# Keys transposed into the raw weights' buffer, tokens loaded first in a segment, value tiles on alternating banks, and memory's answers behind the first projection

## The chip, the cores and the metric

The kernel runs on one core of a Trainium2 chip. The metric is the device time of one execution in microseconds. Before the change three runs gave a median of 693.09 us (692.84 to 693.54).

## The reference

One input x (2048 tokens, 448 features) is normalised and goes through two branches whose results are added to x: an attention with a compressive memory, and a gated linear unit. All is float32.

```python
xn = _layernorm(x)
return x + _A_ref(xn, wq, wk, wv, wo, beta) + _B_ref(xn, w_gate, w_up, w_down)

# A: 16 heads of 28, 4 segments of 512 tokens, one after the other
logits = einsum("bhqd,bhkd->bhqk", qs, ks) * scale + mask      # causal, inside a segment
a_dot = softmax(logits) @ vs
a_mem = (phi(qs) @ M) / (phi(qs) @ z + 1e-6)                   # memory of the earlier segments
o = g * a_mem + (1 - g) * a_dot                                # g = sigmoid(beta), per head
M += phi(ks)^T @ vs;  z += sum(phi(ks))                        # phi(t) = t + 1 or exp(t)
# B: h = sigmoid(xn @ w_gate) * (xn @ w_up);  h @ w_down       # 448 -> 1792 -> 448
```

## The kernel before, in words

Every large product is computed with each operand split into a high and a low part, so one 448-deep product is 11 matmuls (the list TERMS). The program has two stages.

The **front** (lines 282 to 645) goes through the four segments b = 0 to 3 of 512 tokens. In a segment, TensorE computes four value tiles of 128 tokens (`values`, 11 matmuls at L334 each); after the third it updates the memory with the keys and values of the segment before (`update`, 128 small matmuls at L399, reading kn and vst); then it recalls the memory for the queries of the segment before (`recall`, 32 matmuls at L420 on phi, then four DVE transposes at L423); then come seven projections c = 0 to 6 of 128 columns of keys and queries together (`keys_queries`, 11 matmuls at L359 each). Keys are columns 0 to 447, so projections 0 to 2 are keys, 3 is half keys, half queries, and 4 to 6 are queries. In the last segment the order is 3, 4, 5, 6, 0, 1, 2. Between the projections stand the transposes of the next segment's tokens (L97).

What follows each projection: ScalarE copies the high part (L360) and computes the two first steps of phi into a tile e (L364, L365); DVE subtracts for the low part (L366) and finishes e (L368). The pair of parts goes to DRAM (qd, L372). Where the columns are keys, `turn_keys` transposes e in 32 by 32 blocks into a tile `tb` (L383) and four transfers write it to DRAM (kd, L386), from where kn is loaded in token order (L390), in two pieces, after projections 3 and 4. Where the columns are queries, e goes to DRAM (fd, L371), and after projection 6 `phi_queries` loads phi from there in four transfers (L411). The stores of qd for projections 5 and 6 are held back until phi's loads are issued.

The recalled answers of the segment before are handled one per projection: `divide` (DVE L131 to L133, then a multiplication on GpSimd, L134), and one projection later `answer`: a DVE transpose into a `tb` buffer (L430) and a store that GpSimd issues (od, L431).

Buffers around the change: `tb` has three buffers, for keys and answers together; e has three; `stage` is an 8 KB tile that holds the raw weights of projections 0 to 3 at the start and nothing afterwards. The eight PSUM banks are shared by tag: "p", "s" and "gu" two banks each, "m" and "pd" one each. In the first three segments projections use "p" and "gu" by turns, in the last "p" and "s"; value tiles 0 and 1 use "p", 2 and 3 "gu" (in the last segment "s"). The bank of a projection is free when DVE has finished e from it.

The tokens of segment b + 2 (one load of 896 KB into acc, L617) are issued on SyncE after projection 2 of segments 0 and 1. Their first reader is `statistics` (L300) in the next segment.

In the last segment the first steps of the **joint stage** (the gated unit, attention's scores and weights, and the output projection, woven together by a count of steps) already stand between the projections.

In the front the order of TensorE, ScalarE, DVE and SyncE is the written one; GpSimd's is chosen by the planner. In the joint stage TensorE and SyncE keep the written order, and the planner orders the others. A buffer of a tag is chosen by the planner among those that it takes to be free; the first writer waits for the last reader of that buffer.

Of the kernel before, what the change touches and what calls it, by code (L numbers as in the profile page):

```python
# [9 lines left out]
F32 = mybir.dt.float32  # L10
# [6 lines left out]
P = 128  # L17
# [4 lines left out]
NB = 4  # L22
L = 512
# [3 lines left out]
HG = 4  # L27
NG = H // HG
# [35 lines left out]
def kernel(  # L64
# [10 lines left out]
    nc = tc.nc  # L75
# [8 lines left out]
    acc = [keep.tile([P, NT, D], F32, name=f"acc{b}") for b in range(NB)]  # L84
# [27 lines left out]
    def x_block(b):  # L112
        return x[b * L:(b + 1) * L, :].rearrange("(t p) d -> p t d", p=P)
# [5 lines left out]
    def bank(name, tag):  # L119
        return ps.tile([P, L], F32, name=name, tag=tag, bufs=banks[tag])  # L120
# [48 lines left out]
    rest, begin, wo = [], [], {}  # L169
# [112 lines left out]
    with tc.tile_pool(name="front", bufs=2) as sb, tc.manual_schedule(engines=FRONT):  # L282
        stage = eight_k(F32, "stage").rearrange("p (c a) n -> p c (a n)", c=4)
# [56 lines left out]
                nc.sync.dma_start(vd[b], vst.rearrange("p t h d -> p t (h d)"))  # L340

        def values(b, t):
            pv = bank("pv", "p" if t < 2 else "gu" if b < NB - 1 else "s")
            value_terms(b, t, pv, TERMS)
            turned.append(pv)
            if t == 2:
                update(b - 1)
            if t > 1:
                for n in range(len(turned)):
                    store_values(b, t + 1 - len(turned), turned.pop(0))  # L350

        turned = []

        def keys_queries(b, c):

            qk = four_k(F32R, "qk")
            pp = bank("pp", ("p", "gu" if b < NB - 1 else "s")[c % 2])
            for n, (a, w) in enumerate(TERMS):
                T.matmul(pp, wqk[c][:, w, :], xs[b][:, a, :], start=n == 0, stop=n == len(TERMS) - 1)  # L359
            A.activation(qk[:, 0, :], pp, AF.Copy)  # L360
            e = None
            if (c < 4 and b < NB - 1) or (c > 2 and b > 0):
                e = sb.tile([P, L], F32, name="e", bufs=3)
                A.activation(e, pp, AF.Relu, scale=-1.0)  # L364
                A.activation(e, e, AF.Exp, scale=-1.0)  # L365
            V.tensor_sub(qk[:, 1, :], pp, qk[:, 0, :].bitcast(F32))  # L366
            if e is not None:
                V.scalar_tensor_tensor(e, pp, 0.0, e, op0=ALU.max, op1=ALU.add)  # L368
                if c > 2 and b > 0:
                    lo = max(c * P - D, 0)  # L370
                    nc.sync.dma_start(fd[b][lo:(c + 1) * P - D], e[D + lo - c * P:])  # L371
            held.append(lambda: nc.sync.dma_start(qd[b][c * P:(c + 1) * P], qk.bitcast(F32)))  # L372
            if c < 5 or b == 0:
                held.pop()()
            elif c == 6 and b < NB - 1:
                phi_queries(b)
            return e

        def turn_keys(b, c, e):

            n = min(P, D - c * P)
            kt = sb.tile([P, L], F32, name="tb", bufs=3)
            V.transpose(kt[:n], e[:n])  # L383
            for f in range(0, n, 32):
                rows = kd[b][:, c * P + f:c * P + f + 32].rearrange("(t r) k -> r t k", r=32)
                nc.sync.dma_start(rows, kt[f:f + 32].rearrange("r (t k) -> r t k", k=32))  # L386
# [18 lines left out]

        phi_of, held = {}, []

        def phi_queries(b):
            phi_of[b] = sb.tile([P, HG, L], F32, name="phi", bufs=1)
            for i in range(NG):  # L410
                nc.sync.dma_start(phi_of[b][32 * i:32 * i + DH],  # L411
                                  fd[b][i * GW:(i + 1) * GW].rearrange("(j p) n -> p j n", p=DH))
            while held:
                held.pop(0)()

        def recall(b, phi, tag="s"):
            n2 = [bank("n2", t) for t in (tag, tag, "pd", "m")]
            for j in range(HG):
                for i in range(NG):
                    T.matmul(n2[i][32 * j:32 * j + 32], mst[b % 2][32 * i:32 * i + DH, 32 * j:32 * j + 32],  # L420
                             phi[32 * i:32 * i + DH, j], start=True, stop=True, tile_position=(32 * i, 32 * j))
            for i in range(NG):
                V.transpose(phi[:, i], n2[i])  # L423

        def divide(i, phi):
            weigh(sb, phi[:, i], gate[:, i:i + 1], MEM_EPS)

        def answer(b, i, phi):
            tb = sb.tile([P, L], F32, name="e", bufs=3) if b == NB - 1 else sb.tile([P, L], F32, name="tb", bufs=3)
            V.transpose(tb, phi[:, i])  # L430
            nc.gpsimd.dma_start(od[b][P * i:P * (i + 1)], tb)  # L431

# [73 lines left out]
        pv = [bank("pv", t) for t in ("p", "p", "gu", "gu")]  # L506
# [57 lines left out]
        for b in range(NB):  # L564
            last = b == NB - 1
            xn = {}
            if b > 1:
                phi = phi_of[b - 1]
            st = None
            for t in range(3 if b == 0 else 0, NT):  # L570
                if b > 0:
                    values(b, t)
                if 0 < b < NB - 1 and t == 2:
                    st = rstd(*st)
                    for n in range(2):
                        xn[n] = normalise(b + 1, n, *st[n])
                if b > 1 and t == 3:
                    recall(b - 1, phi, "gu" if last else "s")
                    if last:
                        begin[3]()  # L580
                        divide(0, phi)
                if b == 0:
                    split_qk(t)
                if last and t == 0:
                    next(ffn)
                if last:
                    continue
                if t == (3 if b == 0 else 0):
                    st = statistics(b + 1, 0, NT)
                if t == (3 if b == 0 else 2):  # L590
                    A.activation(one, ident[:, 0:1], AF.Exp)
            e = {}
            for k, c in enumerate(LAST if last else range(7)):
                e[c] = keys_queries(b, c)
                if b == 0 and c + 4 < 7:
                    split_qk(c + 4)
                if k < 4 and not last:
                    turn_keys(b, c, e[k])
                if b > 1:
                    i = k + (1 if last else -1)  # L600
                    if 0 < i <= NG:
                        answer(b - 1, i - 1, phi)
                    if 0 <= i < NG:
                        divide(i, phi)
                if last and k == 3:
                    phi_queries(b)
                    phi = phi_of[b]
                if k == 0:
                    if b == 0:
                        st = rstd(*st)  # L610
                    if b == 0:
                        A.activation(gate, gate, AF.Exp, scale=-1.0)
                        V.tensor_scalar_add(gate, gate, 1.0)
                        V.reciprocal(gate, gate)
                        V.tensor_scalar(gate_n, gate, -1.0, 1.0, op0=ALU.mult, op1=ALU.add)
                if k == 2 and b < 2:
                    nc.sync.dma_start(acc[b + 2], x_block(b + 2))  # L617
                if last:
                    if k > 0:
                        next(ffn)  # L620
                    if k > 4:
                        begin[k - 5]()
                    continue
                if k == 3:
                    key_rows(b, 0, 3 * P)
                if k == 4:
                    key_rows(b, 3 * P, D)
                n = k - 1 if b == 0 else k + 1
                if 2 <= n < 6:
                    turn(b + 1, n - 2, xn[n - 2])  # L630
                if 0 <= n < 4 and n not in xn:
                    xn[n] = normalise(b + 1, n, *st[n])
                if b == 2 and k == 2:
                    next(ffn)
            if last:
                for i in range(2):
                    for _ in range(FILLS[i]):
                        next(ffn)
                    if i == 0:
                        recall(b, phi)  # L640
                        for j in range(NG):
                            divide(j, phi)
                    for j in range(2):
                        answer(b, 2 * i + j, phi)
                begin[2]()
# [3 lines left out]
    sb = ctx.enter_context(tc.tile_pool(name="att", bufs=1, reuse_waits="tile"))  # L649
# [207 lines left out]
    with tc.manual_schedule(engines=MANUAL), ExitStack() as joint:  # L857
        next(steps)
        k = sum(FILLS) + 6
# [51 lines left out]
```

## Time and profile before

| | |
|---|---|
| median of 3 runs | 693.09 us |
| profiled execution | 690.35 us, span 688.6 us |
| TensorE busy | 669.9 us (97%) |
| VectorE (DVE) busy | 561.5 us (82%) |
| ScalarE (ACT) busy | 335.0 us (49%) |
| GpSimd (POOL) busy | 169.8 us (25%) |
| mean granted TensorE clock | 0.994 |

Times in the profile are microseconds from the start of the span. PE is TensorE's matmuls, PEld its weight loads, SPq the issuing of transfers on SyncE. A row in order of time gives start, length, engine, line, operation, output and input, and in brackets the idle time before it with what ended it. A row of waits gives total, number and longest. In the chain of waits a row gives start, length and what the chain went through. The front ends at about 153 us; segment 1 starts at 38, segment 2 at 69 and segment 3 at 106 us.

### The profile page before, as it was taken

The numbers are of one execution on the slowest core, as the hardware profiler recorded it, in microseconds if no ns is written. First come the engines' busy times: TensorE is split into PE (matmuls) and PEld (weight loads), VectorE is DVE, ScalarE is ACT, GpSimd is POOL, SyncE is SP. The second block draws the span as 40 slices with busy tenths as digits, with TensorE's granted clock in tenths as the row PEclk, the third lists the DMA queues.
The fourth block names the chain that finished last, engine by engine and source line by source line (L and its number), as shares of the span: only waits on it lengthen the run. The fifth ranks groups of instructions, "written<-read, shape, count | busy, mean of one in ns | idle before, by whom it ended". The sixth has DMA issues, their size and how long they took to land.

```text
span 688.6 us, 11163 instructions
## 1 busy us (share of the span) xinstructions
PE 669.9 (97%) x3915; PEld 551.1 (80%) x3915; DVE 561.5 (82%) x979; ACT 335.0 (49%) x547; POOL 169.8 (25%) x368
## 2 busy tenths in 40 slices
PE   8999994999999999999999999999999999999998
PEld 8788673878778787887878778787887878778897
DVE  6857475457899899997998889899898899888964
ACT  5747362333464455544545555455544556544320
POOL 4402032213222232321331223222222233222000
PEclk9999998999999999999999999999999999999999
DMA  8678978788332432233441343324143423314272
GB/s 267 200 245 238 324 222 249 259 305 237 100 80 57 116 100 70 52 107 94 100 112 45 72 124 65 106 57 115 52 104 93 98 60 81 70 41 122 71 210 103
DMA packets 71567, 89.93 MB, mean 131 GB/s; under 512 B 30168, under 2 KB 46424, under 8 KB 71000
## 3 DMA queue, kind: packets, MB, share of 16 engines
q1 hardware_dynamic: 68504, 81.88, 40.7%
q0 software_dynamic: 3008, 7.34, 5.3%
q8 instruction: 31, 0.51, 0.3%
q14 instruction: 24, 0.20, 0.1%
HBM read 53.81 MB, written 35.39 MB: 130 GB/s over the span
## 4 chain that ended last, share of the span: by engine, by line
PE 82%; DMA 7%; DVE 6%; issue 2%; ACT 1%; POOL 1%; SPq 0%; DVEq 0%; POOLq 0%; ACTq 0%
PE pgu L252 38%; PE pd L178 19%; PE pa L755 5%; PE st L680 5%; PE po L844 5%; PE pp L359 5%; DMA kd<-tb 2%; PE pv L334 2%; DMA fd<-e 2%; DMA od<-tb 1%; PE pv L502 1%; DVE e L368 1%; DVE qk L366 1%; DMA kn<-kd 1%; DMA phi<-fd 1%
## 5 line engine op out<-in xcount | busy, mean ns | idle before, releaser
L252 PE MATMUL pgu<-xs,wgu 128*128 128x512 f32 x1232 | 315.0, 394 | 0.0
L252 PEld LDWEIGHTS pgu<-xs,wgu 128*128 128x128 f32 x1232 | 226.3, 188 | 44.0 <-issue 2.6
L178 PE MATMUL pd<-wdn,hh 128*128 128x448 f32 x672 | 161.5, 367 | 1.4 <-DVE acc L181 1.3
L695 POOL TENSOR_SCALAR_AFFINE_SELECT w<-w 128x256 f32<-128x256 f32 (+1 forms) x160 | 80.8, 507 | 234.8 <-ACT w L684 200.7
L178 PEld LDWEIGHTS pd<-wdn,hh 128*128 128x128 f32 x672 | 123.1, 188 | 16.9 <-DVE acc L181 1.9
L735 ACT ACTIVATE w<-w 128x1024 f32<-128x1024 f32 (+1 forms) x96 | 86.6, 914 | 87.2 <-DVE w L734 85.0
L734 DVE TENSOR_TENSOR w<-w,mb 128x1024 f32<-128x1024 f32 (+1 forms) x96 | 99.6, 1051 | 0.1
L684 ACT ACTIVATE w<-st 128x512 f32<-128x512 f32 x128 | 74.9, 588 | 47.0 <-PE st L680 45.2
L698 DVE TRANSPOSE_TENSOR_REDUCE mx<-w 128x32 f32<-128x1024 f32 x64 | 79.1, 1236 | 13.1 <-POOL w L695 13.0
L359 PE MATMUL pp<-xs,wqk 128*128 128x512 f32 x308 | 74.9, 395 | 0.0
L181 DVE TENSOR_TENSOR acc<-pd,acc 128x448 f32<-128x448 f32 x112 | 67.5, 603 | 1.4 <-PE pd L178 1.4
L359 PEld LDWEIGHTS pp<-xs,wqk 128*128 128x128 f32 x308 | 56.9, 188 | 13.2 <-issue 0.8
L680 PE MATMUL st<-qk 84*128 84x128 f32 (+3 forms) x256 | 63.9, 311 | 0.3 <-ACT w L684 0.2
L263 ACT ACTIVATE hh<-sg 128x512 fp32r<-128x512 f32 x56 | 35.1, 627 | 52.2 <-DVE sg L262 50.9
L680 PEld LDWEIGHTS st<-qk 84*128 84x128 f32 x256 | 48.2, 189 | 8.9 <-ACT w L684 1.3
L260 ACT ACTIVATE sg<-pgu 128x512 f32<-128x512 f32 x56 | 33.2, 592 | 37.5 <-PE pgu L252 36.3
L724 DVE STREAM_TRANSPOSE mb<-top 128x1024 f32<-128x1024 f32 x32 | 39.7, 1240 | 10.9 <-POOL top L721 10.5
L262 DVE SCALAR_TENSOR_TENSOR sg<-sg,pgu 128x512 f32<-128x512 f32 x56 | 37.3, 666 | 3.4 <-PE pgu L252 3.4
L334 PE MATMUL pv<-wv,xs 128*128 128x448 f32 x132 | 30.4, 385 | 9.9 <-DVE e L368 9.9
L267 DVE SCALAR_TENSOR_TENSOR hh<-sg,hh 128x512 fp32r<-128x512 f32 x56 | 38.6, 690 | 1.0 <-ACT hh L263 0.6
L755 PE MATMUL pa<-w,vv 128*32 128x128 f32 (+3 forms) x512 | 38.8, 436 | 0.0
L844 PE MATMUL po<-wo,xs 128*128 128x448 f32 (+2 forms) x187 | 36.3, 352 | 0.0
(100 smaller groups left out, 602.8 us busy)
## 6 DMA issues: line engine op xcount, KB each, us to landing
qk<-qd SPq DMA_DIRECT2D x192, 112.0 KB
qd<-qk SPq DMA_DIRECT2D x28, 512.0 KB
raw<-in_w_ffn SPq DMA_DIRECT2D x14, 512.0 KB
vd<-vst SPq DMA_DIRECT2D x4, 1024.0 KB
vv<-vd SPq DMA_DIRECT2D x16, 256.0 KB
od<-w POOLq DMA_DIRECT2D x16, 256.0 KB, 4.0
ob<-od SPq DMA_DIRECT2D x32, 128.0 KB
out<-acc SPq DMA_DIRECT2D x15, 224.0 KB
```

The lines of the kernel that those rows point to most:

```text
L178: T.matmul(pd[:, :D], l, r, start=n == 0, stop=n == len(mms) - 1)
L181: V.tensor_add(acc[b][:, t, :], pd[:, :D], acc[b][:, t, :])
L252: T.matmul(dst, wgu[f][:, w, side * P:(side + 1) * P], xs[b][:, a, :], start=n == 0, stop=n == len(TERMS) - 1)
L359: T.matmul(pp, wqk[c][:, w, :], xs[b][:, a, :], start=n == 0, stop=n == len(TERMS) - 1)
L680: T.matmul(st[:, at:at + L - kb * P], self.qk[:KS, 1, h, kb * P:(kb + 1) * P], self.qk[:KS, 0, h, kb * P:], start=True, stop=True)
L684: A.activation(w, st, AF.Copy)
L695: G.affine_select(d, d, pattern=pattern, base=0, channel_multiplier=-1, compare_op=ALU.is_ge, fill=MASK)
L698: V.tensor_reduce(mx[:, 16 * (n - 1):16 * (n + 1)], w3[:, n // 2, :2 * L].rearrange("p (b n) -> p b n", n=32), axis=mybir.AxisListType.X, ...
L734: V.tensor_sub(w, w, m)
L735: A.activation(w, w, AF.Exp, scale=SCALE)
L755: T.matmul(pa[32 * j:32 * j + 32, kb * P:], self.vv[:, kb, 32 * j:32 * j + 32], self.pairs[j // 2].block(j % 2, kb), start=kb == 0, stop=k ...
L844: T.matmul(po[:, cols], xs[b][:, a, t * P:(t + 1) * P], out_weights(w)[:, cols], start=m == 0, stop=m == len(TERMS) - 1)
```

## The change

Six things are edited.

1. `turn_keys` transposes into `stage[:, c, :]`, the quarter that held the raw weights of projection c. `tb` is then used by the answers alone and has two buffers instead of three; e has four instead of three.
2. The value tiles take the two tags by turns: "p", "gu", "p", "gu" (last segment: "p", "s", "p", "s").
3. The load of segment b + 2's tokens is issued before projection 0 instead of after projection 2.
4. The recall of the segment before moves from behind the last value tile to behind the matmuls of the first projection, ahead of what ScalarE and DVE do with that projection. In the last segment the first `divide` moves with it.
5. phi's loads 0 and 1 are issued before projection 6 of segments 1 and 2, loads 2 and 3 after it as before; in the last segment all four stay where they were.
6. The release of the held stores becomes a function of its own, called where it happened before.

```diff
         def values(b, t):
-            pv = bank("pv", "p" if t < 2 else "gu" if b < NB - 1 else "s")
+            pv = bank("pv", ("p", "gu" if b < NB - 1 else "s")[t % 2])
...
-        def keys_queries(b, c):
+        def keys_queries(b, c, between=None):
...
                 T.matmul(pp, wqk[c][:, w, :], xs[b][:, a, :], start=n == 0, stop=n == len(TERMS) - 1)
+            if between:
+                between()
             A.activation(qk[:, 0, :], pp, AF.Copy)
...
-                e = sb.tile([P, L], F32, name="e", bufs=3)
+                e = sb.tile([P, L], F32, name="e", bufs=4)
...
             elif c == 6 and b < NB - 1:
-                phi_queries(b)
+                phi_queries(b, 2, NG)
+                release()
...
-            kt = sb.tile([P, L], F32, name="tb", bufs=3)
+            kt = stage[:, c, :]
             V.transpose(kt[:n], e[:n])
...
+        def release():
+            while held:
+                held.pop(0)()
+
-        def phi_queries(b):
-            phi_of[b] = sb.tile([P, HG, L], F32, name="phi", bufs=1)
-            for i in range(NG):
+        def phi_queries(b, i0, i1):
+            if i0 == 0:
+                phi_of[b] = sb.tile([P, HG, L], F32, name="phi", bufs=1)
+            for i in range(i0, i1):
...
-            tb = sb.tile([P, L], F32, name="e", bufs=3) if b == NB - 1 else sb.tile([P, L], F32, name="tb", bufs=3)
+            tb = sb.tile([P, L], F32, name="e", bufs=4) if b == NB - 1 else sb.tile([P, L], F32, name="tb", bufs=2)
...
-                if b > 1 and t == 3:
-                    recall(b - 1, phi, "gu" if last else "s")
-                    if last:
-                        begin[3]()
-                        divide(0, phi)
+                if last and t == 3:
+                    begin[3]()
...
+            def recalls():
+                recall(b - 1, phi, "gu" if last else "s")
+                if last:
+                    divide(0, phi)
+
             e = {}
             for k, c in enumerate(LAST if last else range(7)):
-                e[c] = keys_queries(b, c)
+                if k == 0 and b < 2:
+                    nc.sync.dma_start(acc[b + 2], x_block(b + 2))
+                if 0 < b < NB - 1 and k == 6:
+                    phi_queries(b, 0, 2)
+                e[c] = keys_queries(b, c, recalls if b > 1 and k == 0 else None)
...
                 if last and k == 3:
-                    phi_queries(b)
+                    phi_queries(b, 0, NG)
+                    release()
                     phi = phi_of[b]
...
-                if k == 2 and b < 2:
-                    nc.sync.dma_start(acc[b + 2], x_block(b + 2))
```

More of the change, by code (lines that the diff above doesn't have):

```diff
@@ L406 @@
         phi_of, held = {}, []
-        def phi_queries(b):
-            phi_of[b] = sb.tile([P, HG, L], F32, name="phi", bufs=1)
-            for i in range(NG):
+        def release():
[5 more added lines that the diff above has]
+            for i in range(i0, i1):
                 nc.sync.dma_start(phi_of[b][32 * i:32 * i + DH],
                                   fd[b][i * GW:(i + 1) * GW].rearrange("(j p) n -> p j n", p=DH))
-            while held:
-                held.pop(0)()
         def recall(b, phi, tag="s"):
```

## The prediction

> **What bounds the kernel now.** I read the page first, then who waited for whom on PE, then PE, DVE and SyncE in order of time around the starts of the segments, and the chain of waits there.
>
> ```profile
> span 688.6 us, 11163 instructions
> PE 669.9 (97%) x3915; PEld 551.1 (80%) x3915; DVE 561.5 (82%) x979; ACT 335.0 (49%) x547; POOL 169.8 (25%) x368
> ```
> ```profile
> PE pv L334 <- DVE e L368: 9.9, 3, 7.9
> PE pmm L399 <- DMA kn<-kd: 1.3, 1, 1.3
> ```
>
> PE is the bound: 669.9 of 688.6 us busy. Nearly all that it waits for after the start lies in the attention front, at segment boundaries. In PE's order of time (start, length, instruction, idle before it):
>
> ```profile
> 46.51 0.98 PE L399 MATMUL pmm<-vst,kn 128*32 128x32 f32 x90 [1.33 <-DMA kn<-kd]
> 72.56 4.68 PE L334 MATMUL pv<-wv,xs 128*128 128x448 f32 x22 [0.97 <-DVE e L368]
> 80.81 2.87 PE L420 MATMUL n<-phi,mst 28*32 28x512 f32 x6
> 83.85 1.13 PE L420 MATMUL n<-phi,mst 28*32 28x512 f32 x26 [0.17 <-DMA phi<-fd]
> 84.91 5.33 PE L359 MATMUL pp<-xs,wqk 128*128 128x512 f32 x22
> 99.81 5.28 PE L359 MATMUL pp<-xs,wqk 128*128 128x512 f32 x22
> 106.08 2.48 PE L334 MATMUL pv<-wv,xs 128*128 128x448 f32 x11 [1.00 <-DVE e L368]
> 116.46 6.58 PE L334 MATMUL pv<-wv,xs 128*128 128x448 f32 x22 [7.89 <-DVE e L368]
> 126.61 1.14 PE L420 MATMUL n<-phi,mst 28*32 28x512 f32 x32
> ```
>
> Two losses are not printed as idle. The recall of segment 2 begins at 80.81 and ends at 84.98, 4.17 us, where segment 3's 32 matmuls take 1.14: 3.03 lost, of which 0.17 shows as a wait. And 22 value matmuls take 6.58 after the long wait, 4.68 elsewhere: 1.90 lost to the clock:
>
> ```profile
> 106.00:116.50 10.50, 2.52 (x12) 2.03 (x12) 5.32 (x13) 1.79 (x3) 2.12 (x3) 0.87 0.77 230
> 116.50:123.00 6.50, 6.50 (x26) 5.63 (x27) 1.03 (x1) 0.00 (x0) 0.00 (x0) 0.69 0.98 246
> ```
>
> (Columns: length, busy time of PE, PEld, DVE, ACT, POOL, granted clock, DMA share, GB/s.) The clock falls to 0.69 for the stretch behind the wait.
>
> Why DVE was late at 116.46, from DVE's order of time and the chain of waits:
>
> ```profile
> 97.23 0.67 DVE L430 STREAM_TRANSPOSE tb<-phi 128x512 f32<-128x512 f32 x1
> 102.03 0.70 DVE L383 STREAM_TRANSPOSE tb<-e 64x512 f32<-64x512 f32 x1 [1.43 <-DMA od<-tb]
> 107.67 0.71 DVE L430 STREAM_TRANSPOSE tb<-phi 128x512 f32<-128x512 f32 x1 [1.64 <-DMA od<-tb]
> 114.52 0.71 DVE L430 STREAM_TRANSPOSE tb<-phi 128x512 f32<-128x512 f32 x1 [3.43 <-DMA od<-tb]
> 115.73 0.67 DVE L368 SCALAR_TENSOR_TENSOR e<-pp,e 128x512 f32<-128x512 f32 x1
> ```
> ```profile
> 98.85 3.37 DMA kd<-tb
> 103.64 3.94 DMA od<-tb
> 108.68 5.74 DMA od<-tb
> ```
>
> Keys and memory's answers share the three tb buffers. The last key and two of the answers wait, 6.5 us together, for an earlier answer's store to land; behind them on DVE stands the e of the last projection (L368), and the second value tile of segment 3 takes that projection's bank.
>
> **The change, part by part.**
>
> *Keys into the stage buffer, and tb now for answers alone.* No instruction is added. DVE does the same work between the recall of segment 2 and the last e:
>
> ```profile
> 85.07:116.40 31.33, 22.21 (x104) 17.68 (x104) 22.57 (x47) 14.93 (x26) 10.47 (x12) 0.96 0.79 240
> ```
>
> 22.57 us busy in 31.33. I put the pass without buffer waits at 23.0, with 0.4 of gaps between instructions. Each answer still needs one of two buffers; if they alternate, the third answer waits for the first one's store. Answers come one projection apart, two projections are about 6 us (five start in 99.81 - 84.91 = 14.9), and a store lands 3.94 to 5.74 after its issue, so the wait is near nothing: value 0, bounds 0 and 5 (the first rival). The stage buffer used to be free for the gated unit's first weights from the start; now it comes free when segment 2's last key stores land, and the split that takes it stands on ACT three projections after those keys, behind the last e: 0.
>
> *Value tiles on alternating banks.* The last projection's bank is now taken by the third value tile instead of the second: one tile later, 4.68 / 2 = 2.34. In segment 2 this covers the 0.97. In segment 3 it helps only as far as DVE's pass is shorter. PE after the recall of segment 2: from 84.98 to the end of the last projection at 99.81 + 5.28 = 105.09 are 20.1, less one projection that now stands ahead of the recall (half of 5.33, 2.6) and a 0.3 wait: 17.3; two value tiles make it 22.0. DVE needs 23.0. So **a wait of 1.0 stays** there, with all else in place. The bounds are 0 (POOL and ACT in step, gaps smaller) and 3 (the pass at 25). What falls is 1.00 + 7.89 + 1.90 = 10.8, less 1.0: **9.8**.
>
> *Memory's answers behind the first projection.* The recall moves one projection later: 32 matmuls and four DVE transposes, with the same operands. The four transposes now stand ahead of that projection's subtraction on DVE, which frees its bank; the next user of the bank is four projections on, over 10 us, so nothing waits. In segment 3 the two "gu" banks of the recall are next taken by a gated matmul one projection later (2.6) instead of two; the transposes that free them come first on DVE (2.51 for four), so this costs 0, at most 1. What it gives in segment 2 depends on when phi lands. From the chain:
>
> ```profile
> 34.81 7.00 DMA kd<-tb
> 73.67 5.11 DMA fd<-e
> 79.19 4.53 DMA phi<-fd
> ```
>
> Phi landed at 83.72. Without the 0.97 the recall will be asked for at 80.81 - 0.97 + 2.6 = 82.4. So 1.3 us must still come from the chain, else they stay.
>
> *Tokens first, four e buffers, phi's first half earlier.* The 896 KB of tokens move from behind the third projection to ahead of the first, one SyncE issue each, past fifteen stores of keys and queries (the rows are SyncE's, in order of time):
>
> ```profile
> 33.20 0.51 SPq L617 DMA_DIRECT2D acc<-in_x  x1
> 64.39 0.39 SPq L617 DMA_DIRECT2D acc<-in_x  x1
> 72.44 0.37 SPq L390 DMA_DIRECT2D kn<-kd  x1
> 72.91 1.14 SPq L371 DMA_DIRECT2D fd<-e  x2
> ```
> ```profile
> 17.20:26.00 8.80, 8.80 (x41) 7.36 (x40) 6.10 (x18) 8.11 (x17) 5.24 (x5) 1.00 0.50 188
> 46.00:52.00 6.00, 5.49 (x111) 4.91 (x112) 1.62 (x6) 3.33 (x6) 0.62 (x2) 1.00 0.26 103
> 65.00:70.00 5.00, 5.00 (x24) 4.18 (x23) 3.47 (x6) 3.45 (x7) 0.00 (x0) 1.00 0.85 255
> ```
>
> They now fall where the transfers are half idle (shares 0.50 and 0.26) and leave the crowded stretch (0.85); 0.92 MB at its 255 GB/s is 3.6 us, an estimate from this row. The stores that they pass come up to 3.6 later; only kn, two projections on, reads them, so this is hidden, and if kn came as much later the update would wait 1.3 as now. In segment 0 the last key store, issued behind the tokens, took 7.00 and set the 1.33 wait of the memory update; 3.6 less covers it: **1.3 gained**, bounds 0 and 1.3. The tokens' own reader, the statistics of the next segment, is 20 us off. In segment 1 the second kn load at 72.44 waited for a key store issued behind the tokens and held the fd stores of projections 5 and 6 back to 72.91; both come about 2 us earlier. A fourth e buffer takes away ACT's wait for a store ahead of the last e. Against this, phi's loads 0 and 1 now stand ahead of the last fd store on SyncE and wait there for projection 5's store: behind them are that last fd store, phi's loads 2 and 3, the held query stores and the next value store. If a store takes 5.11 the last fd store goes out later by about 5 less the 2.5 of one projection, so the chain gains 2 and loses up to 2.5. I take 2 us better and 0.7 worse: 1.3, just what is needed. So **3.0 gained, less 0.7 for safety**: 2.3, bounds 0.5 and 3.0.
>
> The same order costs in segment 3, where the recall had no wait. Time from the end of segment 2's recall: e of projection 5 at 23.0 - 2.1 (one answer, one pair of L366 and L368) = 20.9, its store landing 3.4 (the row at 98.85) to 5.1 later, then the last fd store as long again, then phi 4.5: 32.2 to 35.6. PE asks for it at 23.0 + two value tiles 4.7 + update 1.3 + projection 2.6 = 31.6. So **a new wait of 0.6 to 4.0**; the transfer share in segment 2's middle is below that of the crowded rows and SyncE holds back for DVE there, so I take 1.0.
>
> **The sum**, against the profiled execution's 690.35: 9.8 (segment 3's start) + 1.0 (segment 2's bank) + 2.3 (segment 2's recall) + 1.3 (update) - 1.0 (segment 3's recall) = 13.4, and 0.5 off for the gated stage's first loads, which find the transfers busier: 12.9. 690.35 - 12.9 = 677.4. The three timed runs had a median of 693.09, 2.7 above the profiled one; against these **680.2**. Behind the front PE hardly waits, so nothing there can absorb the gain as long as DVE keeps up:
>
> ```profile
> PE pd L178 <- DVE acc L181: 1.3, 1, 1.3
> PE st L680 <- ACT w L684: 0.2, 1, 0.2
> ```
>
> **Two rules of the skill.** The Trainium skill, "TensorE: Matmul & The Clock Gate", section "What's actually happening", says that an idle window of about 3.4 us puts the array at half clock until it has been busy as long. The trace agrees, with 0.69 behind a 7.89 us wait. By it waits of 1 us cost no clock, and the first rival's wait would cost some 1.7 us more, an estimate from that page. The Trainium skill, "SBUF — State Buffer", section "SBUF: two separate sides", speaks against a denser DVE: a transfer started by GpSimd can sit without descriptors while VectorE holds the port they share. The store issued at 108.68 took 5.74 though DVE was idle for its last 3.4 us, so the trace does not bear this out; by the rule the answers' stores would land late, the first rival would hold, and the time would be 685 to 687 instead of 680.
>
> **The rivals.**
> 1. *Answers still go one after the other*: each next answer's buffer is the one that the answer before it still stores from, as the third and fourth did (1.64, 3.43). For it: that is what the rows at 107.67 and 114.52 show with three buffers; against it: with keys gone a free buffer stands by. A period of 0.7 + 0.3 + 3.94 to 5.74 per answer, over about 4 for the DVE work of one projection: 1 to 2.7 thrice, some 5 more on the pass. Gain 12.9 - 5 = 7.9, and a clock loss of up to 1.9: 685 to 687.
> 2. *Transfers are the bound*: the share from 52 to 164 us is high already.
>
> ```profile
> 52.00:164.00 112.00, 101.60 (x771) 79.94 (x771) 68.03 (x140) 50.60 (x89) 22.40 (x28) 0.97 0.85 264
> 164.00:650.00 486.00, 484.39 (x2598) 396.12 (x2597) 436.21 (x704) 250.53 (x395) 129.40 (x310) 1.00 0.34 87
> ```
>
>    0.85 of 112 in some 100 us is 0.95. Then segment 2's recall keeps its 3.0, segment 3's waits 4.0 and the gated stage's first tiles another 1: 12.9 - 2.3 - 3.0 - 0.5 = 7.1, so 686.
> 3. *The gain is given back in the joint stage*: DVE is 436 of 486 us busy there (90%); if ACT and DVE get another order, small waits could add up to the gain: 693. Against it: two waits, 1.5 us, in 520 us now.
> 4. *Slower*: stage is one buffer of four parts. If a key's transpose must wait until all of the previous key's four stores have landed, each one after the first waits: the third key's transpose ends where the row at 97.23 begins, its stores land at 98.85 + 3.37 = 102.22, so 5 us against a projection's 3, 2 us more three times in each of segments 0, 1 and 2. It decides once the 6 us exceed the 2.34 of the moved bank and the update's slack: some 3.5 in each of segments 1 and 2, kn and phi 6 late with 3 more each, and DVE's pass in segment 2 at 29, which leaves 4 of the 9.8: 690.35 + 13 - 4 = 699, timed about 702. Against it: the first statistics, of one part of a token tile, start at 3.38, and the load of its last part only goes out at 4.04, so waits go by parts, for loads at least:
>
> ```profile
> 3.38 0.64 DVE stats L300
> 4.04 0.43 SPq L437 DMA_DIRECT2D acc<-in_x  x1
> ```
>
> **How the numbers follow.** Forecast (gain 10 to 15) 0.56, rival 1 0.14, rival 2 0.16, rival 3 0.05, rival 4 0.06, better still 0.03. The forecast's own range: 678 to 683. For 8 in 10 the range takes in rivals 1 and 2: **677 to 687**. About 0.2% (1.4 us) tells a change from none here: faster 0.56 + 0.14 + 0.16 + 0.03, rounded to 0.88; same 0.05; slower 0.07.
>
> **What would show it.** Right: no wait of DVE at L430 or L383 on a store; the third value tile of segment 3 waits 1 us, with no stretch of low clock; the recall of segment 2 takes 1.1 to 2 us; no wait of the memory update in segment 1; the front some 13 us shorter and the waits after it unchanged. Wrong: L383 waiting for kd stores, PE waiting at L420 by 3 us, or new waits after 200 us.

## The result and the profile after

The changed kernel takes 688.02 us (median of 4 runs, 686.61 to 688.88) against 693.32 us (4 runs): a ratio of 0.9922, 95% interval 0.9903 to 0.9940. It is faster by 5.3 us. The forecast was 12.9 us, 680.2, with a range of 677 to 687: the direction was right, the gain less than half, and the time 1 us outside the range. The profiled execution took 688.34 us (span 686.6), 2.0 less than the one before; that one had been 2.7 below its runs, this one is 0.3 above.

Who waited for whom on PE, changed kernel (total, number, longest):

```profile
PE n L426 <- DMA phi<-fd: 4.2, 3, 2.8
PE pmm L402 <- DMA kn<-kd: 3.1, 2, 1.9
PE pv L334 <- DVE e L370: 0.3, 1, 0.3
```

The waits for DVE's e went from 9.9 us to 0.3, as meant. The recall (now L426) and the memory update (L402) wait for transfers instead. PE in order of time, changed kernel:

```profile
44.86 1.30 PE L402 MATMUL pmm<-vst,kn 128*32 128x32 f32 x128
77.01 0.98 PE L402 MATMUL pmm<-vst,kn 128*32 128x32 f32 x90 [1.90 <-DMA kn<-kd]
80.24 2.70 PE L359 MATMUL pp<-xs,wqk 128*128 128x512 f32 x11
82.87 1.19 PE L426 MATMUL n<-phi,mst 28*32 28x512 f32 x4
86.91 3.06 PE L426 MATMUL n<-phi,mst 28*32 28x512 f32 x28 [2.84 <-DMA phi<-fd]
89.89 4.41 PE L359 MATMUL pp<-xs,wqk 128*128 128x512 f32 x11
113.89 2.48 PE L334 MATMUL pv<-wv,xs 128*128 128x448 f32 x11 [0.32 <-DVE e L370]
118.02 0.98 PE L402 MATMUL pmm<-vst,kn 128*32 128x32 f32 x90 [1.17 <-DMA kn<-kd]
123.88 1.05 PE L426 MATMUL n<-phi,mst 28*32 28x512 f32 x4
126.09 1.04 PE L426 MATMUL n<-phi,mst 28*32 28x512 f32 x2 [1.17 <-DMA phi<-fd]
127.34 1.94 PE L426 MATMUL n<-phi,mst 28*32 28x512 f32 x26 [0.21 <-DMA phi<-fd]
129.21 3.59 PE L359 MATMUL pp<-xs,wqk 128*128 128x512 f32 x11
152.01 1.14 PE L426 MATMUL n<-phi,mst 28*32 28x512 f32 x32
```

The recall of segment 2 runs from 82.87 to 89.97, 7.10 us for work of 1.14, and the projection behind it takes 4.41 instead of 2.70. That of segment 3 takes 5.40 (123.88 to 129.28), the projection behind it 3.59. The last row is the recall that ends the front: it starts at 152.01; before it started at 152.16. In the profiled pair the front is as long as before; what moved lies inside it:

| in the front, us | before | after | gained |
|---|---|---|---|
| update of segment 1 waits | 1.33 | 0 | 1.3 |
| bank at segment 2's second value tile | 0.97 | 0 | 1.0 |
| update of segment 2 waits | 0 | 1.90 | -1.9 |
| recall of segment 2, beyond 1.14 | 3.03 | 5.96 | -2.9 |
| projection behind it, beyond 2.70 | 0 | 1.71 | -1.7 |
| start of segment 3, waits and clock | 10.8 | 0.3 | 10.5 |
| update of segment 3 waits | 0 | 1.17 | -1.2 |
| recall of segment 3, beyond 1.14, and the projection behind it | 0 | 4.26 + 0.89 | -5.2 |
| sum | | | -0.1 |

The 2.0 us of the profiled pair that are left come at and behind the end of the front, where PE's wait at L178 fell from 1.3 to 0.3. Where the other 3 us of the timed 5.3 come from, no profile shows.

The clock in these stretches (length, busy time of PE, PEld, DVE, ACT, POOL, granted clock, DMA share, GB/s), changed kernel:

```profile
77.00:84.00 7.00, 6.99 (x116) 5.19 (x116) 1.62 (x6) 4.36 (x8) 0.62 (x2) 1.00 0.28 77
89.80:94.20 4.40, 4.40 (x25) 3.39 (x13) 4.12 (x7) 0.00 (x0) 0.00 (x0) 0.59 0.49 205
127.30:132.60 5.30, 5.26 (x37) 3.05 (x38) 3.19 (x8) 0.00 (x0) 0.00 (x0) 0.68 1.01 403
```

The second row is the projection behind the late recall of segment 2, at a clock of 0.59; the third is the end of segment 3's recall and the projection behind it, at 0.68. The first row is the clue to the cause: while the store that segment 2's recall waits for is under way, **the transfers are mostly idle**, busy for 0.28 of the time. So it is not their throughput that PE waits for there. SyncE's order of time and the chain of waits, changed kernel, show what it is:

```profile
69.05 0.37 SPq L393 DMA_DIRECT2D kn<-kd  x1
69.52 1.03 SPq L373 DMA_DIRECT2D fd<-e  x1
73.93 4.07 SPq L419 DMA_DIRECT2D phi<-fd  x2
78.05 0.39 SPq L373 DMA_DIRECT2D fd<-e  x1
83.72 0.75 SPq L419 DMA_DIRECT2D phi<-fd  x2
```
```profile
69.05 7.92 DMA kn<-kd
78.05 5.60 DMA fd<-e
83.72 3.14 DMA phi<-fd
```

phi's load 1 stands at SyncE until the fd store of projection 5, issued at 69.52, has landed, and goes out at 77.68. Behind it stands the last fd store, whose e DVE had finished by 70.5; it goes out at 78.05, **7.5 us late**, needs 5.60, and only then can phi's loads 2 and 3 be issued.

DVE itself did what was forecast. Between the start of the recall's transposes and the end of the last e:

```profile
90.05:113.84 23.79, 23.26 (x104) 18.97 (x104) 22.22 (x46) 13.32 (x23) 10.56 (x12) 0.93 0.82 241
```

23.8 us where the forecast had 23.0 and before it were 31.3, with no wait for a tb buffer.

### The profile page after: what moved, and what is told of

Same layout as the page of the kernel before. It is cut to its first block, busy times and chain, and to the rows that moved or that the text cites. A ratio compares the mean times of both kernels' runs of the same rounds, so it can differ in the third digit from the quotient of the medians.

```text
span 686.6 us, 11158 instructions
## 1 busy us (share of the span) xinstructions
PE 672.7 (98%) x3915; PEld 551.4 (80%) x3915; DVE 561.1 (82%) x979; ACT 336.2 (49%) x547; POOL 167.2 (24%) x368
## 4 chain that ended last, share of the span: by engine, by line
PE 79%; DMA 10%; DVE 6%; issue 1%; SPq 1%; ACT 1%; POOL 1%; ACTq 0%; DVEq 0%; POOLq 0%
PE pgu L252 38%; PE pd L178 19%; PE pa L766 5%; PE st L691 5%; PE po L855 5%; PE pp L359 3%; DMA kn<-kd 2%; DMA fd<-e 2%; DMA qd<-qk 2%; DMA kd<-stage 1%; PE pv L334 1%; DMA stage<-in_w_qk 1%; DMA phi<-fd 1%; DMA acc<-in_x 1%; DMA gate<-in_beta 1%
## 5 line engine op out<-in xcount | busy, mean ns | idle before, releaser
L178 PE MATMUL pd<-wdn,hh 128*128 128x448 f32 x672 | 161.4, 367 | 0.3 <-DVE acc L181 0.3
L706 POOL TENSOR_SCALAR_AFFINE_SELECT w<-w 128x256 f32<-128x256 f32 (+1 forms) x160 | 78.1, 489 | 241.8 <-ACT w L695 204.3
L178 PEld LDWEIGHTS pd<-wdn,hh 128*128 128x128 f32 x672 | 123.1, 188 | 15.7 <-issue 1.0
L359 PE MATMUL pp<-xs,wqk 128*128 128x512 f32 x308 | 77.7, 404 | 0.0
L359 PEld LDWEIGHTS pp<-xs,wqk 128*128 128x128 f32 x308 | 58.7, 194 | 15.4 <-issue 3.3
L362 ACT ACTIVATE qk<-pp 128x512 fp32r<-128x512 f32 x28 | 16.7, 598 | 47.1 <-PE pp L359 40.4
```

Of the source, the lines that this page charges most:

```text
L178: T.matmul(pd[:, :D], l, r, start=n == 0, stop=n == len(mms) - 1)
L706: G.affine_select(d, d, pattern=pattern, base=0, channel_multiplier=-1, compare_op=ALU.is_ge, fill=MASK)
```

## The experiments

Ratios are against the kernel before, run beside it on the same chip. Where two experiments are compared, it is by their ratios; 0.001 is 0.7 us.

### phi's loads together again

The changed kernel without its fifth edit.

```diff
-                if 0 < b < NB - 1 and k == 6:
-                    phi_queries(b, 0, 2)
...
-                phi_queries(b, 2, NG)
+                phi_queries(b, 0, NG)
```

> The changed kernel with phi's four loads together after projection 6 again, behind the last fd store; all else as changed. Theory A (order on SyncE: the last fd store stood behind the wait of phi's load 1, issued at 78.05 instead of about 70.5 in segment 2): the recalls of segments 2 and 3 wait under 1 us each, the two stretches of low clock go, and 688.0 becomes 679 to 682. Theory B (the transfers themselves are the bound of the front, whatever their order): within 1 us of 688.0. Theory C (the recall's new place is what costs, through DVE): within 2 us of 688.0, with the recall still late.

679.95 us (6 runs), ratio 0.9811 (0.9780 to 0.9842). Theory A holds: taking back this one edit gives some 8 us, clear of the changed kernel's interval. That the time is also that of the forecast, 680.2, is partly chance, since the waits are not the forecast's. SyncE and PE in order of time, this kernel:

```profile
69.55 2.35 SPq L373 DMA_DIRECT2D fd<-e  x2
73.89 5.11 SPq L419 DMA_DIRECT2D phi<-fd  x4
```
```profile
77.12 1.06 PE L402 MATMUL pmm<-vst,kn 128*32 128x32 f32 x90 [2.29 <-DMA kn<-kd]
78.11 3.93 PE L334 MATMUL pv<-wv,xs 128*128 128x448 f32 x11
84.46 1.14 PE L426 MATMUL n<-phi,mst 28*32 28x512 f32 x32
113.69 0.98 PE L402 MATMUL pmm<-vst,kn 128*32 128x32 f32 x90 [2.28 <-DMA kn<-kd]
119.53 1.71 PE L426 MATMUL n<-phi,mst 28*32 28x512 f32 x32
143.19 1.14 PE L426 MATMUL n<-phi,mst 28*32 28x512 f32 x32
```

Both fd stores go out by 71.9, all of phi by 79.0, and the recall of segment 2 takes 1.14. The end of the front comes at 143.2 instead of 152.0. The update still waits for kn, 2.3 us in each of segments 2 and 3. Of what theory A named, two things came only in part: the value tile behind the first of these waits is slow (3.93 for 2.48), so a stretch of low clock stayed, and the recall of segment 3 takes 1.71.

### The same, with 0.92 MB more to transfer

```diff
+                if k == 2 and b == 1:
+                    nc.sync.dma_start(spare, x_block(0))
```

(spare is a buffer in DRAM that nobody reads; the copy is from DRAM to DRAM.)

> As phi_whole, with one transfer added: 0.92 MB of tokens copied from DRAM to a spare DRAM buffer, issued on SyncE in segment 1 after projection 2, in the crowded part; nobody reads it. Theory B: 2.4 to 3.6 us more than phi_whole, the transfer time of 0.92 MB. Theory A: no more than 1.5 us above phi_whole, since the chain has slack when it is not held on SyncE.

682.98 us (6 runs), ratio 0.9843 (0.9813 to 0.9873). 3.0 us more by the medians, in the range of theory B, but 2.2 by the ratios, between the two theories, and the intervals overlap: the times alone do not decide. In the profiles the updates' waits for kn are 6.9 us here against 4.6. That points to bytes in this crowded part costing time through kn, once the order on SyncE is mended.

### phi's loads issued by GpSimd

```diff
-                nc.sync.dma_start(phi_of[b][32 * i:32 * i + DH],
+                nc.gpsimd.dma_start(phi_of[b][32 * i:32 * i + DH],
```

(on top of phi_whole)

> As phi_whole, but phi's loads are issued by GpSimd, so that their waits hold nothing on SyncE. Theory A: as phi_whole or up to 2 us faster (678 to 682), the last fd store and the held query stores go out at once. Theory B: 687 to 688.

685.96 us (6 runs), ratio 0.9894 (0.9861 to 0.9926): 6 us slower than phi_whole, a miss for what both theories had expected. In the profiles about half of it is there before the recall that ends the front, which starts at 146.61 for 143.19: the updates wait 5.3 for kn instead of 4.6, and value tiles behind these waits are slow in both segments (4.06 and 3.96). Most of the rest is that recall's own wait. GpSimd and PE in order of time and the chain of waits, this kernel:

```profile
137.91 0.57 POOL L437 DMA_DIRECT2D od<-tb  x1 [1.04 <-DVE tb L436]
138.49 1.79 POOL L419 DMA_DIRECT2D phi<-fd  x3
```
```profile
146.61 1.15 PE L426 MATMUL n<-phi,mst 28*32 28x512 f32 x4
149.93 1.51 PE L426 MATMUL n<-phi,mst 28*32 28x512 f32 x26 [0.52 <-DMA phi<-fd]
```
```profile
140.27 9.52 DMA phi<-fd
```

GpSimd issues phi's loads behind the last answer's store, from 138.49; on SyncE (phi_whole) they went out from 134.28. Since the recall itself is asked for 3.4 later here, the issue is late by only some 0.8. The last load then took 9.52 to land, with the transfers busy all the time (1.01 from 141 to 146 us). Which of the transfers held it is not shown.

### The split alone, on the kernel before

The fifth edit and nothing else.

```diff
+                if 0 < b < NB - 1 and k == 6:
+                    phi_queries(b, 0, 2)
...
-                phi_queries(b)
+                phi_queries(b, 2, NG)
+                release()
```

> The kernel before with one edit alone: phi's loads 0 and 1 ahead of projection 6 in segments 1 and 2. Theory A: the last fd store goes out 5 us or more late in segment 2 and the recall of segment 2 waits some 4 us longer, while segment 3 hides it behind DVE's wait of 7.89: 695 to 699. If the split is harmless: within 1 us of 693.3.

695.84 us (7 runs), ratio 1.0054 (1.0032 to 1.0077): slower by itself, by 3.7 us, as theory A had it (695 to 699). Chain of waits and PE, this kernel:

```profile
78.93 3.31 DMA fd<-e
82.30 3.19 DMA phi<-fd
```
```profile
81.19 1.61 PE L424 MATMUL n<-phi,mst 28*32 28x512 f32 x4
85.53 3.14 PE L424 MATMUL n<-phi,mst 28*32 28x512 f32 x28 [2.73 <-DMA phi<-fd]
121.53 7.10 PE L334 MATMUL pv<-wv,xs 128*128 128x448 f32 x22 [7.50 <-DVE e L368]
```

The last fd store goes out at 78.93 (72.91 with its neighbour before); segment 2's recall takes 7.5 us instead of 4.2. In segment 3 the wait for DVE is there as before, and the recall behind it takes its 1.14.

### The other parts, taken back one at a time from phi_whole

Keys and answers in three shared tb buffers, three e buffers:

```diff
-            kt = stage[:, c, :]
+            kt = sb.tile([P, L], F32, name="tb", bufs=3)
...
```

> phi_whole (the changed kernel with phi's four loads together again, 680.0) with keys and answers back in three shared tb buffers and three e buffers. By the prediction's steps the keys' own buffer carries most of the 9.8 of segment 3's start: DVE waits at L386 and L436 for stores by 5 to 7 us, the third value tile of segment 3 waits 3 to 6, and the clock falls behind it: 684 to 689. If the other parts cover it: 680 to 681.

686.50 us (4 runs), ratio 0.9917 (0.9887 to 0.9947): 7 us lost, the largest part. DVE waits for answers' stores as before, and PE with it:

```profile
115.95 3.86 PE L334 MATMUL pv<-wv,xs 128*128 128x448 f32 x11 [6.37 <-DVE e L370]
```

Value tiles 0 and 1 on "p", 2 and 3 on "gu":

```diff
-            pv = bank("pv", ("p", "gu" if b < NB - 1 else "s")[t % 2])
+            pv = bank("pv", "p" if t < 2 else "gu" if b < NB - 1 else "s")
```

> phi_whole with value tiles 0 and 1 on p and 2 and 3 on gu again. By the prediction's steps the second value tile then waits for the last e: 2.3 more in segment 3 and 1.0 in segment 2: 682 to 684. If kn sets the update's time anyway (it waits 2.3 in segments 2 and 3 in phi_whole), the wait only moves ahead of the update: 680 to 681.

678.39 us (4 runs), ratio 0.9801 (0.9762 to 0.9839): no loss, where the prediction's steps would have had 682 to 684. The wait came back where it was expected (PE waits 0.35 and 2.53 us for e at L334), but the update behind it then waits 0.3 for kn instead of 4.6. The wait is only taken at another place.

The recall ahead of the first projection:

```diff
-                e[c] = keys_queries(b, c, recalls if b > 1 and k == 0 else None)
+                e[c] = keys_queries(b, c)
```

(with the call of recall, begin[3] and divide back behind the fourth value tile)

> phi_whole with the recall ahead of the first projection again. By the prediction's steps phi is then asked for 2.6 earlier: in segment 2 up to 2.6 lost, in segment 3 up to 2.6, together 681 to 685, with PE waiting at the recall's matmuls. If the recall's place does nothing for the wait but delays DVE (theory C): 679 or less.

683.04 us (4 runs), ratio 0.9869 (0.9838 to 0.9900): 4 us lost, as expected for two segments; the interval just touches that of phi_whole. PE waits at the recall again:

```profile
82.38 2.78 PE L426 MATMUL n<-phi,mst 28*32 28x512 f32 x32
120.77 1.99 PE L426 MATMUL n<-phi,mst 28*32 28x512 f32 x28 [1.15 <-DMA phi<-fd]
```

The tokens behind projection 2, once from the changed kernel and once from phi_whole:

```diff
-                if k == 0 and b < 2:
-                    nc.sync.dma_start(acc[b + 2], x_block(b + 2))
...
+                if k == 2 and b < 2:
+                    nc.sync.dma_start(acc[b + 2], x_block(b + 2))
```

> The changed kernel with the load of the tokens back behind projection 2; all else as changed. If the tokens' new place gave what I had put down (1.3 in segment 1 and about 2 on the chain to phi): 690 to 692, with a wait of the memory update in segment 1 of 1 to 3 us. Theory B: 688, the same bytes in the same time.

689.80 us (12 runs), ratio 0.9950 (0.9928 to 0.9973).

> phi_whole with the tokens' load back behind projection 2. By the prediction's steps the update of segment 1 waits 1.3 again and the chain to kn and phi in segment 2 is up to 2 later: 682 to 684. K2: 680, the same bytes.

682.05 us (4 runs), ratio 0.9864 (0.9822 to 0.9907). Both are some 2 to 4 us slower than with the tokens first; neither interval is clear of that of the same kernel with the tokens first. The update's wait in segment 1 is back in both (1.35 and 1.44 us).

### What still waits: kn

Two ways to meet the update's waits of 2.3 us in phi_whole. First, the update behind the fourth value tile:

```diff
-            if t == 2:
+            if t == 3:
                 update(b - 1)
-            if t > 1:
+            if t == 3:
```

> phi_whole with the memory update behind the fourth value tile instead of the third, so that kn may land 2.4 us later; the four value stores follow it. In phi_whole the update waits 2.3 for kn in segments 2 and 3, and the next value tile takes 3.86 instead of 2.48 (clock). If kn's landing is the bound: waits under 0.5, but the first projection waits about 0.7 for its bank in each segment: 675 to 678. If the wait only moves on to phi or the bank: 679 to 681.

679.76 us (4 runs), ratio 0.9827 (0.9789 to 0.9865): no gain. (The 3.86 in the expectation is that tile's length in the chain of waits; in order of time it is the 3.93 shown above.) The update's waits fall to 0.6 and 0.4, and the wait moves on: 1.7 us for the first projections' banks, and recalls of 3.72 and 2.88 us.

Second, the query stores of projections 3 and 4 held back until phi's loads are out:

```diff
-            if c < 5 or b == 0:
+            if c < (5 if b == NB - 1 else 3) or b == 0:
                 held.pop()()
```

> phi_whole with the query stores of projections 3 and 4 of segments 1 and 2 held back too, until phi's loads are out. K1 (kn, fd and phi are late because they stand behind query stores of 512 KB in the transfer queue): kn lands 1.5 to 3 earlier, the update's waits fall under 1 us, 676 to 678. K2 (the front is bound by its bytes, in whatever order): the waits move, 679 to 682.

675.68 us (4 runs), ratio 0.9764 (0.9721 to 0.9806). PE in this kernel:

```profile
74.52 1.30 PE L402 MATMUL pmm<-vst,kn 128*32 128x32 f32 x128
80.67 2.65 PE L426 MATMUL n<-phi,mst 28*32 28x512 f32 x32
109.81 0.98 PE L402 MATMUL pmm<-vst,kn 128*32 128x32 f32 x90 [1.11 <-DMA kn<-kd]
115.62 2.18 PE L426 MATMUL n<-phi,mst 28*32 28x512 f32 x32
```

kn is in time in segment 2 and 1.1 late in segment 3. By the medians 4 us better than phi_whole, by the ratios 3; the intervals of the two overlap, that of the changed kernel (0.9903 to 0.9940) is clear of both. Explanation K1, that kn stands behind query stores in the transfer queue, fits the update's waits; the recalls take 2.65 and 2.18 here. This version beats both kernels: 16 us below before by its ratio.

Both edits together:

> Both edits together. K1: no wait for kn or phi in segments 2 and 3, 674 to 677; if the first projection's bank is the next bound, no better than the better of the two. K2: 679 to 682.

676.71 us (4 runs), ratio 0.9782 (0.9746 to 0.9818): not told apart from the better of the two. No update or recall of segments 2 and 3 waits for a transfer by the profile's list of waits; 1.7 us of waits for the first projections' banks and 1.3 for a gated matmul's bank stand in their place, and the recall of segment 3 still takes 2.74.

## Why the prediction was wrong

**The step that failed** is "Tokens first, four e buffers, phi's first half earlier", where it says that the chain "gains 2 and loses up to 2.5. I take 2 us better and 0.7 worse". The mechanism stood there, with what is queued behind the waiting load, but its size was wrong. It assumed that the fd store of projection 5 goes out one projection, 2.5, before the last e and lands 5.11 after its issue. It went out only 1.0 before (69.52 for 70.5), behind kn's second load, and phi's load 1, which waits for it, could go out 8.2 after it, at 77.68. So the last fd store went out 7.5 us after its e, not 2.5. That kn's loads and a query store ahead of it made the store of projection 5 that slow is argued: where two query stores of each segment are held back (hold_queries), the updates' waits for kn fall. Segment 2's recall lost 5.96 beyond its work, not 0.7, and the clock took 1.71 more behind it. In segment 3 the same step gave "a new wait of 0.6 to 4.0", of which 1.0 was taken; it was 4.3, and 0.9 more by the clock. In the terms of the sum, up to the end of the front: 6.9 less than forecast at segment 2's recall (4.6 lost for 2.3 gained), 4.2 less at segment 3's (5.2 lost for 1.0), 3.1 less at the updates, and 0.7 more at segment 3's start, so that of 13.4 nothing is left. Taking the edit back gives some 8 us. The time is then the forecast's own partly by luck: 4.6 us of waits for kn that the forecast did not have stand against recalls of 1.14 and 1.71 that wait less than it had taken, and more is gained behind the front than the forecast had.

**The update.** The 1.3 of segment 1 came. That the updates of segments 2 and 3 would wait, 1.90 and 1.17, was not in the sum: the moved tokens bring kn's second load out at 69.05 instead of 72.44, but it lands 7.92 later, so nearly all of the head start was lost in the transfer queue while PE itself had become earlier. When kn lands in segments 2 and 3 stood in no part of the argument. The forecast had the tokens leave a crowded stretch, a share of 0.85 from 65 to 70 us; with them gone, and the work there 1.4 us earlier, the share in these 5 us was 0.90. It should have been asked what that does to kn.

**Right:** keys in their own buffer (DVE's pass 23.8 for 23.0; 7 us when it is taken back from phi_whole); one answer's buffer is free when the next needs it, so rival 1 did not happen; the residual wait at the third value tile (0.32 for 1.0); the recall's place (4 us in two segments, by intervals that just touch; the forecast's step had 2.3 in one); the gated stage behind the front, which gave nothing back (0.7 us of waits behind 164 us, before 1.5), so rival 3 is out; and no wait of a key's transpose on the stage buffer, so rival 4 is out. The alternating banks gave nothing that can be measured in phi_whole (0.9801 without them, 0.9811 with): the 1.0 put down for segment 2 goes to kn instead.

**Rival 2** came within 2 us, 686, with the waits about where it put them, but mostly for another reason. While the last fd store was under way the transfers were 0.28 busy in segment 2, and 0.38 from 119 to 124 us in segment 3; PE waited for a store that had been issued late. Crowded transfers come in ahead of that: the store of projection 5, for which it stood back, landed in a stretch with a share of 0.85 (69.05 to 77.00 us). The update's waits are those of a crowded queue, as the added 0.92 MB and the held query stores indicate, though not clear of noise.

**The clock.** In segment 2 the recall's longest wait was 2.84 us, and the clock still fell to 0.59 behind it. In segment 3 no wait of the update or the recall was longer than 1.17, and the clock was 0.68 behind them. The Trainium skill, "TensorE: Matmul & The Clock Gate", section "What's actually happening", gives about 3.4 us of idle as the limit; here it fell behind shorter waits that stand among small matmuls, and also behind one of 2.29 in phi_whole, where the next value tile took 3.93. Taken with the few matmuls between the waits, the stretches of the recalls are longer: 82.87 to 86.91 with four matmuls, 123.88 to 127.34 with six. So the rows do not tell a shorter limit from small matmuls that count for little. The forecast's sentence that waits of 1 us cost no clock fits the single waits ahead of value tiles (0.97 and 1.00 before, with the tiles at their usual 4.68 and 2.48). It does not fit segment 3's recall, where waits of 1.17 and 0.21 among its matmuls were followed by a projection of 3.59 for 2.70.

## What to carry to other kernels

In this kernel a load that had to wait for an earlier store held everything behind it on its issuing queue, above all the store that the next load needed (7.5 us here, 8 us of the whole time). So issue all stores of a chain before the first load that waits, even if an early load could start sooner. Price such a wait by how long that store takes when it is really issued, behind everything that is queued then, not by the shortest row. And where a wait is taken from one engine, ask at each later wait whether what it waits for has become earlier by as much as the engine has.

## What was not expected of the hardware

The last fd store, issued at 78.05, took 5.60 us to land while the transfers were 0.28 busy; before it took 5.11 in a crowded stretch (share 0.96 from 69.20 to 84.95 us), and with the split alone 3.31. Changed kernel, the last part of its 5.60 (same columns as above):

```profile
81.00:83.70 2.70, 2.70 (x13) 1.52 (x11) 0.00 (x0) 0.92 (x3) 0.00 (x0) 1.00 0.05 15
```

A mean share of 0.05 over 16 engines is less than the full time of one of them, so for about half of its time the store was not held by full transfers. What held it is not settled. And waits of 2.1 to 2.5 us before the second part of the update were in some kernels followed by a slow value tile (4.06 after a wait of 2.14 in phi_pool, 3.93 after 2.29 in phi_whole, 3.78 after 2.46 in whole_keys_back), but not in phi_whole's segment 3 (a wait of 2.28, then 2.48).
